# A fused sigmoid-attention and SwiGLU kernel: first unit in two parts, a refitted scheduler model, four units loaded ahead of the weights

## The chip, the cores and the metric

The kernel runs on one core of a Trainium2 chip. The metric is the device time of one execution in microseconds (us); lower is better. A comparison takes the executions of the same rounds on the same chip. The kernel before took 443.03 us (median of 3, 442.38 to 443.8).

## The reference, cut to what matters

```python
# q, k, v: (8, 12, 448, 64) float32
scores = q @ k.T / sqrt(64) - log(448)
attn   = 1 / (1 + exp(-scores))            # a sigmoid, no softmax
x      = (attn @ v) as (3584, 768)         # heads side by side
g, val = x @ w_gate, x @ w_val             # (768, 1536) each
out    = (g * sigmoid(g) * val) @ w_out    # (1536, 768)
```

The work falls into 24 **units** of four heads; three units make one batch's input of the feed-forward part.

## The kernel before: the parts that matter

A unit is loaded in three transfers (q, k, v; a transfer is a DMA) and cast to 16 bits. q and k of the first six units are transposed on TensorE (PE) and copied from PSUM, the buffers that hold TensorE's results here; those of the later units go through a DMA transpose. In the profiles PEld is TensorE's loading of weights, DVE is VectorE, POOL is GpSimd and SP issues most of the transfers. Then come seven score groups of four 64 x 64 matmuls, each with its sigmoid on ScalarE (ACT), and 28 small matmuls with v (P·V), evicted as the tiles `xT`. Feed-forward group `f` of a batch takes six gate and six value matmuls of 128 x 128 weights.

```python
slots = {"A": 2, "TO": 2, "G": 2, "st": 11, "src": 2, "v16": 3, "qkT": 3, ...}   # buffers of each kind
# A: scores.  TO: transposes, P.V and outputs share these two.  G: gate and value.  st: staging of loads.

ORDER = "q1 q2 w0 q3 w1 q4 w2 q5 w3 q6".split()     # q3: unit 3's loads; w0: a quarter of gate and value weights

loads(0)
cast_qk(0, "q", None, [("DVE", 0, 4), ("ACT", 4, NS)])
tr_pe(0, 0)
cast_qk(0, "k", None, [("DVE", 0, 4), ("ACT", 4, NS)])
tr_pe(0, 1)
```

Every operation is an object with an engine, a modelled duration, what it depends on and which buffers it takes and gives. A list scheduler in the program plays these through on a model of the core and fixes the order in which each engine's instructions are issued. So a constant of the model is no time: it can only change an order.

```python
LAT = {"PE": 0.2, "ACT": 0.1, "DVE": 0.08, "POOL": 0.25, "SP": 2.2}
...
for o in list_schedule(ops, slots, window):   # sorted by modelled start
    o.fn()
```

## Time and profile before

| | before |
|---|---|
| time, median of 3 | 443.03 us |
| span of the profiled execution | 441.6 us |
| TensorE busy / idle in it | 424.7 / 16.9 us |
| first sigmoid | 8.20 us |
| third unit's last sigmoid ends, fourth unit's first starts | 30.75, 34.13 us |
| first whole feed-forward group starts | 34.45 us |

The prediction below shows the views that carry this. Beside them stand three rows of the timeline of the kernel before (start, length, engine, line, operation; in brackets the idle time just before and what ended it). They are the place where the fourth unit comes late:

```profile
31.84 0.94 PE L282 MATMUL ps_tr<-idn,src 128*128 128x128 bf16 x14 [0.66 <-ACT xT L195]
...
34.13 1.90 ACT L329 ACTIVATE pt<-ps_sc,sbiast 128x896 f16<-128x896 f32 x2 [0.40 <-PE ps_sc L315]
34.45 1.29 PE L381 MATMUL ps_g<-xT,wg 128*128 128x448 f16 x6 [0.24 <-DVE t L391]
```

The fourth unit's 14 transposes wait for the third unit's eviction on ACT, since both need the two shared PSUM buffers. ACT therefore has no scores for over 3 us, and TensorE itself pauses twice.

### The profile page before, as it was taken

To read this page: it belongs to the slowest core of one execution; us is meant where nothing else is said; L and a number is where in the kernel's file an instruction comes from. 1 tells how busy PE (TensorE), PEld (TensorE's weight loads), DVE (VectorE), ACT (ScalarE), POOL (GpSimd) and SP (SyncE) were. 2 spreads that over 40 slices of the span, in tenths; PEclk is the share of its full clock that TensorE was granted. 3 is DMA by queue.
4 is the path that set the end of the run, shared out by engine and by line. 5 is a ranking of instruction groups with operands and counts; after the bars stand their busy time and mean duration, and the time that the engine had idled before them with its cause. 6 is when DMAs were issued, how large, how long until landed. Compare 5 with 4: busy or idle time off the path is not lost.

```text
span 441.6 us, 7888 instructions
## 1 busy us (share of the span) xinstructions
PE 424.7 (96%) x3252; PEld 211.4 (48%) x3252; DVE 168.5 (38%) x278; ACT 224.9 (51%) x305; POOL 127.8 (29%) x193
## 2 busy tenths in 40 slices
PE   3879999999999999999999999999999999999995
PEld 1444444444555545444455444544444545554563
DVE  2425543454343333434343423434333433344210
ACT  4787778756464464546545465365654452111111
POOL 2688746643230431304322403404100000000000
PEclk9999999999999999999999999999999999999999
DMA  8999989998077275265666644535410111120144
GB/s 280 378 377 376 323 251 309 309 307 255 1 203 167 72 203 127 78 133 121 154 141 115 186 106 120 181 49 165 68 37 11 27 37 37 36 71 1 43 101 108
DMA packets 64196, 66.97 MB, mean 152 GB/s; under 512 B 35488, under 2 KB 60320, under 8 KB 64160
## 3 DMA queue, kind: packets, MB, share of 16 engines
q1 hardware_dynamic: 62432, 59.39, 47.5%
q0 software_dynamic: 1728, 7.08, 7.1%
q8 instruction: 25, 0.41, 0.4%
q14 instruction: 11, 0.09, 0.1%
HBM read 47.19 MB, written 11.01 MB: 132 GB/s over the span
## 4 chain that ended last, share of the span: by engine, by line
PE 92%; ACT 3%; DMA 2%; DVE 1%; issue 1%; SPq 0%; ACTq 0%
PE ps_g L381 25%; PE ps_v L381 25%; PE ps_o L439 19%; PE ps_sc L315 9%; PE ps_pv L347 7%; PE ps_ol L439 5%; ACT pt L329 2%; DMA st_q<-in_q_dram 2%; PE ps_tr L282 1%; DVE t L391 1%; ACT s L387 1%; SPq L211 0%; DVE src L197 0%; ACT xT L195 0%; DVE osb L452 0%
## 5 line engine op out<-in xcount | busy, mean ns | idle before, releaser
L329 ACT ACTIVATE pt<-ps_sc,sbiast 128x896 f16<-128x896 f32 x168 | 159.3, 1005 | 26.1 <-PE ps_sc L315 26.0
L381 PE MATMUL ps_g<-xT,wg 128*128 128x448 f16 x576 | 125.0, 353 | 1.1 <-DVE t L391 1.0
L381 PE MATMUL ps_v<-xT,wv 128*128 128x448 f16 x576 | 125.5, 354 | 0.0
L387 ACT ACTIVATE s<-ps_g 128x448 f16<-128x448 f32 x96 | 52.2, 543 | 120.7 <-PE ps_g L381 120.7
L391 DVE TENSOR_TENSOR t<-ps_g,s 128x448 f16<-128x448 f32 x96 | 59.9, 624 | 125.5 <-ACT s L387 125.5
L439 PE MATMUL ps_o<-wo,hT 128*128 128x384 f16 x528 | 92.5, 326 | 0.0
L439 PEld LDWEIGHTS <-hT 128*128 128x128 f16 x672 | 65.7, 98 | 45.8
L397 DVE SCALAR_TENSOR_TENSOR hT<-ps_v,t 128x448 f16<-128x448 f32 x96 | 59.9, 624 | 60.2 <-PE ps_v L381 58.5
L381 PEld LDWEIGHTS <-wg 128*128 128x128 f16 x576 | 54.7, 98 | 56.7 <-issue 9.6
L381 PEld LDWEIGHTS <-wv 128*128 128x128 f16 x576 | 51.0, 98 | 61.7 <-issue 22.2
L460 POOL DMA_DIRECT2D out_dram<-osb x36 | 18.7, 525 | 134.6 <-issue 112.4
L315 PE MATMUL ps_sc<-qkT 64*64 64x448 bf16 x672 | 51.9, 374 | 4.0 <-ACT pt L329 3.2
L199 POOL CAST v<-st_v 64x448 f16<-64x448 f32 (+1 forms) x72 | 41.0, 569 | 32.6 <-PE ps_pv L347 17.6
L347 PE MATMUL ps_pv<-pt,v 64*64 64x448 f16 x672 | 38.4, 360 | 0.6 <-ACT pt L329 0.5
L199 POOL CAST src<-st_q 128x896 bf16<-128x896 f32 x21 | 19.6, 931 | 59.9 <-DMA st_q<-in_q_dram 38.2
L197 DVE CAST xT<-ps_pv 128x448 f16<-128x448 f32 x40 | 23.4, 619 | 22.9 <-PE ps_pv L347 22.9
L315 PEld LDWEIGHTS <-qkT 64*64 64x64 bf16 x672 | 14.2, 107 | 36.0 <-issue 33.4
L450 ACT ACTIVATE osb<-ps_o 128x384 f32<-128x384 f32 x22 | 10.8, 490 | 39.8 <-PE ps_o L439 39.8
L347 PEld LDWEIGHTS <-v 64*64 64x64 f16 x672 | 19.9, 109 | 15.7 <-issue 5.2
L439 PE MATMUL ps_ol<-wo,hT 128*128 128x384 f16 x144 | 24.7, 326 | 0.0
L452 DVE TENSOR_SCALAR osb<-ps_o 128x384 f32<-128x384 f32 x22 | 12.3, 557 | 31.8 <-PE ps_o L439 31.8
L199 POOL CAST src<-st_k 128x896 bf16<-128x896 f32 x21 | 19.6, 932 | 5.0 <-DMA st_k<-in_k_dram 4.3
(22 smaller groups left out, 68.7 us busy)
## 6 DMA issues: line engine op xcount, KB each, us to landing
st_q<-in_q_dram SPq DMA_DIRECT2D x24, 448.0 KB, 5.0
st_k<-in_k_dram SPq DMA_DIRECT2D x24, 448.0 KB, 5.2
st_v<-in_v_dram SPq DMA_DIRECT2D x24, 448.0 KB, 5.9
out_dram<-osb POOLq DMA_DIRECT2D x36, 192.0 KB, 3.1
st_wg<-in_moe_w_gate_dram SPq DMA_DIRECT2D x12, 384.0 KB, 8.8
st_wv<-in_moe_w_val_dram SPq DMA_DIRECT2D x12, 384.0 KB, 8.8
st_wo<-in_moe_w_out_dram SPq DMA_DIRECT2D x12, 384.0 KB, 6.8
out_dram<-osb SPq DMA_DIRECT2D x18, 192.0 KB, 2.7
```

The lines of the kernel that those rows point to most:

```text
L197: nc.vector.tensor_copy(out=o, in_=i)
L199: nc.gpsimd.tensor_copy(out=o, in_=i)
L315: nc.tensor.matmul(out=sc[64 * (g ^ a):64 * (g ^ a) + 64, a, 0:S].rearrange("k (s p) -> k s p", s=NS), lhsT=kT[r, s, 64 * g:64 * g + 64], ...
L329: nc.scalar.activation(out=pt, in_=T[("sc",) + key][:, :, 0:S], func=SIGM, bias=sb_t, scale=qkscale)
L347: nc.tensor.matmul(out=T["pv", i, a][64 * g:64 * g + 64, :], lhsT=T["v16", i][r, a, s, :], rhs=T["pt", i, s][r, a, :], start=(s == 0), sto ...
L381: nc.tensor.matmul(out=T[nm, b, f], lhsT=w[c][:, j, ff * 128:(ff + 1) * 128], rhs=T["xT", b, j], start=(j == 0), stop=(j == KC - 1))
L387: nc.scalar.activation(out=t, in_=T["g", b, f], func=SIGM)
L391: nc.vector.tensor_tensor(out=t, in0=T["g", b, f], in1=T["s16", b, f], op=MULT)
L397: nc.vector.scalar_tensor_tensor(out=T["hT", m, f][:, o * S:(o + 1) * S], in0=T["v", b, f], scalar=HSC, in1=T["t1", b, f], op0=MULT, op1=MULT)
L439: nc.tensor.matmul(out=o, lhsT=T["hT", m, f][:, t * 128:(t + 1) * 128], rhs=wo16[f][:, cs], start=(f == 0), stop=(f == NF - 1))
L452: nc.vector.tensor_scalar_mul(T["osb", m, t][:, c], o, HREC)
L460: dma.dma_start(out=out[rows, c].rearrange("(p s) d -> s p d", s=NS)[s], in_=T["osb", m, t][64 * n:64 * n + 64, c])
```

## The change

Its intent is to start earlier and to have attention work at hand while the first weights are still on their way. It has four parts.

**Split.** The first unit's k is loaded in two parts, its second half is cast on POOL, and transposes and copies go by parts, so that the first scores need only three sevenths of k.

```diff
-            load(i, nm, src)
+            load(i, nm, src, [0, 3, NS] if i == 0 and nm == "k" else None)
...
-    cast_qk(0, "q", None, [("DVE", 0, 4), ("ACT", 4, NS)])
-    tr_pe(0, 0)
-    cast_qk(0, "k", None, [("DVE", 0, 4), ("ACT", 4, NS)])
-    tr_pe(0, 1)
+    cast_qk(0, "q", None, [("DVE", 0, 4, 0), ("ACT", 4, NS, 0)])
+    tr_pe(0, 0, [("DVE", 0, 4), ("ACT", 4, NS)])
+    cast_qk(0, "k", None, [("DVE", 0, 3, 0), ("POOL", 3, NS, 1)])
+    tr_pe(0, 1, [("DVE", 0, 3), ("DVE", 3, NS)])
```

**Model.** Latencies, durations and the cost of a transfer are refitted (about a dozen more like these).

```diff
-LAT = {"PE": 0.2, "ACT": 0.1, "DVE": 0.08, "POOL": 0.25, "SP": 2.2}
-SWITCH = 0.1
+LAT = {"PE": 0.2, "ACT": 0.15, "DVE": 0.13, "POOL": 0.25, "SP": 2.2}
+SWITCH = 0.094
...
+    R["st_v", 0][0].dma += 1.5
```

**Loading order** and **issue order.** Four units stand ahead of the first weights; P·V of the first units is issued a slot later, and the fourth unit's transposes between the third's scores, no longer after its P·V.

```diff
-ORDER = "q1 q2 w0 q3 w1 q4 w2 q5 w3 q6".split()
+ORDER = "q1 q2 q3 w0 q4 w1 w2 q5 w3 q6".split()
...
-            if sl == 3 and i < QB:
+            if sl == 0 and 0 < i < QB:
+                pv(i - 1)
+            if sl == 3 and i == QB - 1:
                 pv(i)
-            if att and i + 1 < NPE:
-                if i == QB - 1:
-                    if sl == 3:
-                        tr_pe(i + 1, 0)
-                        tr_pe(i + 1, 1)
-                elif sl in (1, 2):
-                    tr_pe(i + 1, sl - 1)
+            if att and i + 1 < NPE and sl in (1, 2):
+                tr_pe(i + 1, sl - 1)
```

More of the change, by code (lines that the diff above doesn't have):

```diff
@@ L36, in __init__ @@
         self.hold = n == 1792
-        self.dma = 2.0 if n == 1792 else n / 16 * max(0.042, 0.0105 + size / 27200)
+        self.dma = 2.0 if n == 1792 else n / 16 * max(0.042, 0.0093 + size / 28700)
     def got(self, tag):
         return [s for s in self.take if s.tag == tag]
-LAT = {"PE": 0.2, "ACT": 0.1, "DVE": 0.08, "POOL": 0.25, "SP": 2.2}
-SWITCH = 0.1
+LAT = {"PE": 0.2, "ACT": 0.15, "DVE": 0.13, "POOL": 0.25, "SP": 2.2}
+SWITCH = 0.094
 START = {"SP": 0.75, "POOL": 1.4, "DVE": 3.4, "ACT": 0.75}
-ORDER = "q1 q2 w0 q3 w1 q4 w2 q5 w3 q6".split()
+ORDER = "q1 q2 q3 w0 q4 w1 w2 q5 w3 q6".split()
 AHEAD = 7
@@ L203, with load, part, fn @@
     R = {}
-    def load(i, nm, src):
+    def load(i, nm, src, cuts=None):
         b, r = divmod(i, QB)
-        def fn():
-            T["st_" + nm, i] = stg.tile([128, 2, NS, D], FP32, tag="st", bufs=slots["st"], name=f"st_{nm}{i}")
-            nc.sync.dma_start(
-                out=T["st_" + nm, i].rearrange("q a s d -> q a (s d)"),
-                in_=src[b][4 * r:4 * r + 4].rearrange("(a g) (p s) d -> (g p) a (s d)", a=2, s=NS))
-        R["st_" + nm, i] = [op("SP", 0.5, fn, take=["st"], desc=(256, NS * D * 4))]
+        def part(s0, s1):
+            def fn():
+                if s0 == 0:
+                    T["st_" + nm, i] = stg.tile([128, 2, NS, D], FP32, tag="st", bufs=slots["st"],
+                                                name=f"st_{nm}{i}")
+                nc.sync.dma_start(
+                    out=T["st_" + nm, i][:, :, s0:s1].rearrange("q a s d -> q a (s d)"),
+                    in_=src[b][4 * r:4 * r + 4].rearrange("(a g) (p s) d -> (g p) a (s d)", a=2, s=NS)
+                    [:, :, s0 * D:s1 * D])
+            return op("SP", 0.5, fn, take=["st"] if s0 == 0 else [], desc=(256, (s1 - s0) * D * 4))
+        cuts = cuts or [0, NS]
+        R["st_" + nm, i] = [part(*c) for c in zip(cuts, cuts[1:])]
     def cast_qk(i, nm, eng, parts=None):
         n = "qk".index(nm)
-        parts = parts or [(eng, 0, NS)]
+        parts = parts or [(eng, 0, NS, -1)]
         def fn(e, s0, s1):
@@ L223, in fn @@
                               T["st_" + nm, i][:, :, s0:s1])
+        one = {"DVE": 0.65, "ACT": 0.95, "POOL": 0.95}
         R["c" + nm, i] = [
-            op(e, (1.05 if e == "DVE" else 0.98) * (s1 - s0) / NS, fn(e, s0, s1), deps=R["st_" + nm, i],
+            op(e, 0.07 + one[e] * (s1 - s0) / NS, fn(e, s0, s1), deps=[R["st_" + nm, i][ld]],
                take=["src"] if nm == "q" and s0 == 0 else [],
                give=R["st_" + nm, i][0].take if s1 == NS else [])
-            for e, s0, s1 in parts]
+            for e, s0, s1, ld in parts]
     def cast_v(i, eng):
@@ L236, in fn @@
                 cp(eng, t[64 - 64 * g:128 - 64 * g, 1], T["st_v", i][64 * g:64 * g + 64, 1])
-        R["v16", i] = op(eng, 1.75, fn, deps=R["st_v", i], take=["v16"], give=R["st_v", i][0].take)
+        R["v16", i] = op(eng, 1.9, fn, deps=R["st_v", i], take=["v16"], give=R["st_v", i][0].take)
     def load_w(w, dst, c, j2, nm):
@@ L275, in qkT_tile, with tr_pe, fpe, fn @@
         T["qkT", i] = sb.tile([128, 2, NS, 128], BF16, tag="qkT", bufs=slots["qkT"], name=f"qkT_{i}")
-    def tr_pe(i, n):
-        def fpe():
-            ps = T["tr", i, n] = psum.tile([128, NS, 128], BF16, tag="TO", bufs=2, name="ps_tr")
-            for s in range(NS):
-                nc.tensor.transpose(out=ps[:, s, :],
-                                    in_=src16[i % NSRC][:, n, s].rearrange("p a d -> p (a d)"), identity=idn)
-        def fm():
-            if n == 0:
-                qkT_tile(i)
-            nc.vector.tensor_copy(out=T["qkT", i][:, n], in_=T["tr", i, n])
-        a = op("PE", 0.4, fpe, deps=R[("cq", "ck")[n], i], take=["TO"],
-               give=R["cq", i][0].take if n else [])
-        m = op("DVE", 0.62, fm, deps=[a], take=["qkT"] if n == 0 else [], give=a.take)
-        R.setdefault(("qkT", i), []).append(m)
+    def tr_pe(i, n, parts=None):
+        ins = R[("cq", "ck")[n], i]
+        parts = parts or [("DVE", 0, NS)]
+        def fpe(s0, s1):
+            def fn():
+                if s0 == 0:
+                    T["tr", i, n] = psum.tile([128, NS, 128], BF16, tag="TO", bufs=2, name="ps_tr")
+                for s in range(s0, s1):
+                    nc.tensor.transpose(out=T["tr", i, n][:, s, :],
+                                        in_=src16[i % NSRC][:, n, s].rearrange("p a d -> p (a d)"),
+                                        identity=idn)
+            return fn
+        def fm(eng, s0, s1):
+            def fn():
+                if n == 0 and s0 == 0:
+                    qkT_tile(i)
+                cp(eng, T["qkT", i][:, n, s0:s1], T["tr", i, n][:, s0:s1])
+            return fn
+        for k, (eng, s0, s1) in enumerate(parts):
+            a = op("PE", 0.06 * (s1 - s0), fpe(s0, s1), deps=[ins[min(k, len(ins) - 1)]],
+                   take=["TO"] if s0 == 0 else [], give=R["cq", i][0].take if n and s1 == NS else [])
+            if s0 == 0:
+                bank = a.take
+            m = op(eng, 0.1 + (0.53 if eng == "DVE" else 0.8) * (s1 - s0) / NS, fm(eng, s0, s1), deps=[a],
+                   take=["qkT"] if n == 0 and s0 == 0 else [], give=bank if s1 == NS else [])
+            R.setdefault(("qkT", i), []).append(m)
+            R["qkT", i, n, s0] = m
     def tr_dma(i):
@@ L320, in burst @@
         give = [x for i, s in ds if s == NS - 1 for x in R["qkT", i][0].got("qkT")]
-        a = op("PE", 0.19 * len(ds), fpe, deps=[x for i in {i for i, _ in ds} for x in R["qkT", i]],
+        deps = [x for i in {i for i, _ in ds} for x in R["qkT", i]]
+        if ds[0][0] == 0:
+            deps = [x for k, x in R.items() if k[:2] == ("qkT", 0) and len(k) > 2 and (k[2] == 0 or k[3] <= ds[0][1])]
+        a = op("PE", 0.03 + 0.19 * len(ds), fpe, deps=deps,
                mode=("Q", "Q"), take=["A"] * len(ds), give=give)
@@ L331, in fn @@
             T[("pt",) + key] = pt
-        R[("pt",) + key] = op("ACT", 0.95, fn, deps=[a], take=["pt"], give=[slot])
+        R[("pt",) + key] = op("ACT", 0.89, fn, deps=[a], take=["pt"], give=[slot])
     def pv(i):
@@ L369, in pv @@
         for g in range(2):
-            R["xT", b, 2 * r + g] = op(eng[g], 0.62, fx(g), deps=[a], take=["xT"], give=[banks[g]])
+            R["xT", b, 2 * r + g] = op(eng[g], 0.54, fx(g), deps=[a], take=["xT"], give=[banks[g]])
     def f1(b, f):
@@ L410, in f1 @@
         g, bank = product(wg16, "g", [])
-        s = op("ACT", 0.5, fs, deps=[g])
-        t = op("DVE", 0.6, ft, deps=[s], give=bank)
+        s = op("ACT", 0.45, fs, deps=[g])
+        t = op("DVE", 0.54, ft, deps=[s], give=bank)
         def val():
@@ L419, in val @@
             old = [R["f2", m - 2]] if m >= 2 and b % 2 == 0 else []
-            R["hT", b, f] = op("DVE", 0.62, fh, deps=[vv, t] + old, give=bank)
+            R["hT", b, f] = op("DVE", 0.54, fh, deps=[vv, t] + old, give=bank)
         return val
```

## The prediction

The landing of k's first part at "about 4.8" is 4.09 + 0.57 = 4.66 and an allowance of 0.1 us. The 0.15 us for a change between 64-row and full matmuls is my estimate from the round at 40.98.

"Half clock", or "cold clock", is told by durations here: in the kernel before, seven transposes took 0.93 us at 4.58 and 0.56 us at 20.27, while the granted-clock column read 1.00 for both.

> **What bounds the kernel now.** I read the page first: busy shares, then the forty slices.
>
> ```profile
> PE 424.7 (96%) x3252; PEld 211.4 (48%) x3252; DVE 168.5 (38%) x278; ACT 224.9 (51%) x305; POOL 127.8 (29%) x193
> ...
> PE   3879999999999999999999999999999999999995
> ...
> DMA  8999989998077275265666644535410111120144
> ```
>
> TensorE is busy 424.7 of 441.6 us, so it waits 16.9 us in all. The row of slices (11 us each) shows where: the first three and the last. Nothing that leaves the matmuls alone can save more than those gaps and some cold clock. Next I cut the span at the events that matter (columns: stretch, length, then busy time of PE, PEld, DVE, ACT, POOL, granted clock, DMA share, GB/s):
>
> ```profile
> 4.58:8.20 3.62, 2.49 (x22) 1.68 (x23) 1.58 (x3) 0.54 (x3) 0.00 (x0) 1.00 0.96 311
> 8.20:14.60 6.40, 4.10 (x34) 1.99 (x30) 3.04 (x5) 4.83 (x6) 4.00 (x6) 1.00 1.05 383
> 14.60:20.00 5.40, 5.37 (x55) 3.08 (x54) 1.78 (x3) 4.15 (x5) 3.86 (x7) 1.00 1.07 373
> 20.00:26.30 6.30, 4.49 (x68) 2.28 (x67) 2.40 (x4) 6.30 (x8) 4.91 (x7) 1.00 1.06 377
> 26.30:33.60 7.30, 6.07 (x70) 3.07 (x66) 1.78 (x3) 5.21 (x7) 6.24 (x10) 1.00 1.06 377
> 33.60:60.00 26.40, 26.09 (x243) 12.52 (x244) 14.48 (x24) 18.99 (x25) 20.23 (x27) 1.00 0.92 305
> ```
>
> Length less PE busy gives idle: 1.13, 2.30, 0.03, 1.81, 1.23 and 0.31 us, together 6.8. To these come 4.58 us before the first transpose and 5.1 us of the last 32.6, where only the last evictions and writes remain. From 33.6 us on TensorE practically never waits. The waits say for whom, and the timeline where (start, length, engine, line; in brackets the idle time before and its releaser):
>
> ```profile
> PE ps_tr L282 <- DVE src L197: 5.8, 3, 4.6
> PE ps_sc L315 <- ACT pt L329: 3.2, 6, 0.7
> ...
> 8.20 2.80 ACT L329 ACTIVATE pt<-ps_sc,sbiast 128x896 f16<-128x896 f32 x3 [2.26 <-PE ps_sc L315]
> 8.87 2.19 POOL L199 CAST v<-st_v 128x448 f16<-128x448 f32 x3 [7.53 <-DMA st_v<-in_v_dram]
> ...
> 10.02 0.63 DVE L197 CAST src<-st_q 128x896 bf16<-128x896 f32 x1 [2.52 <-DMA st_q<-in_q_dram]
> ...
> 17.51 11.17 ACT L329 ACTIVATE pt<-ps_sc,sbiast 128x896 f16<-128x896 f32 x12 [1.13 <-PE ps_sc L315]
> ...
> 19.09 0.67 PEld L282 LDWEIGHTS <-src 128*128 128x128 bf16 x7 [0.38 <-DVE xT L197]
> ...
> 20.27 0.56 PE L282 MATMUL ps_tr<-idn,src 128*128 128x128 bf16 x7
> ```
>
> So the head is a chain: load, cast, transpose, copy, scores, sigmoid; then one sigmoid per 0.93 us (11.17 over 12), 6.5 us per unit of seven, beside DMA at full rate. The first feed-forward matmul stands at 26.31. The first unit's sigmoids start at 8.20, the second's only at 17.51, and the third's end at 30.75. Then ACT starts no sigmoid until 34.13, because the fourth unit is transposed at 31.84, after the third unit's output is evicted.
>
> [...]the granted-clock column reads 1.00: seven transposes took 0.93 us at 4.58 and at 19.09, 0.56 us at 20.27. TensorE was first busy without a gap from 14.63. [...]here a cast of 896 elements took 0.93 us on POOL and 0.63 on DVE.
>
> **The change part by part.** The order of instructions in the built program shows TensorE's count unchanged; SP, POOL and DVE get one instruction more each. Tensor work is only moved.
>
> *First unit in parts.* The whole k landed at 5.43, 1.34 us after q at 4.09. The first 3/7 of it should land 0.57 us after q[...], about 4.8. DVE's cast of 384 elements, interpolated from 0.43 us for 512 and 0.63 for 896, is 0.36 us: done at 5.2. TensorE finishes q's transposes at 5.51 as before (0.93 us from 4.58), then takes three of k, 0.4 us at that clock: 5.9. Add 0.26 us, the distance from 5.51 to the copy at 5.77, and some 0.35 us for half a copy: 6.5. Scores start at about 6.6 in place of 7.56, the first sigmoid at about 7.2 in place of 8.20. Gain **1.0 us** at that point. q's copy, shared by DVE and ACT, ends near 6.25 and doesn't bind. POOL's cast of the rest of k, 4/7 of 0.93, costs nothing: POOL was idle to 8.87.
>
> *What is left of it at the second unit.* Its q still lands at about 10.0 and its k at 11.2, since as many bytes lie ahead of them. Before, the second unit's first scores stood behind five steps of the first unit's P·V (14.96 to 17.1); now two score groups stand ahead of it. Transposes of k at 12.6 to 13.5, copy to 14.3, scores to 14.9: first sigmoid near 15.0, 2.5 us earlier. But P·V then starts at 15.3, still at half clock (20 matmuls 2.1 us), and with two score tiles in PSUM the third sigmoid waits until about 18.0: the lead is two sigmoids (1.9 us) less 0.5. The two banks shared by P·V, transposes and outputs bring small waits again before the fourth and fifth. By the end of the second unit I have 23.7 where the kernel before had 24.0. So most of the first lead is spent: TensorE at half clock, not the load, limits 14 to 20 us. I keep **0.3 us**, with up to 1.5 if the bank waits are milder.
>
> *Four units ahead of the weights.* q3 moves ahead of the first weight chunk. By landings of 1.2 us per unit tensor (10.02, 11.22, 12.54) and 1.0 per weight tile, the fourth unit lands from 17.4 to 19.8, not 23.6 to 26.05, and the chunk from 20.8 to 25.9, not up to 22.35. Casting its last piece ends near 26.7. The value product wants it after that and moves behind the third unit's P·V in the order; the gate product needs its half by 28, cast by 24.1. In return the fourth unit is transposed between the third's scores, in gaps where TensorE waited for ACT (1.81 us of 6.30), and its first two score groups run as soon as the third unit's sigmoids end. So the 3.4 us without sigmoids shrink to under 1. Work that stood on the saturated path after 31.84 disappears from it: the fourth unit's 14 transposes (0.94 us) and eight score matmuls (0.57 us). Against that, four value matmuls (0.93 us) move from a gap to the busy stretch. Adding a wait of 0.24 us at 34.45 that goes: 0.94 + 0.57 - 0.93 + 0.24, about 0.8, and up to 1.6 if the value matmuls too fall beside the evictions: I take **1.5 us**.
>
> *The refitted model.* It reorders everything, but from 33.6 to 409 us there are 1.1 us of idle, 1.0 of them before gate products late in the kernel, and that part of the order is unchanged (the last 100 groups of matmuls, of 367, are the same). Changes between 64-row and full matmuls on TensorE are 182, not 180; four more lie in the head, so two fewer later. One round of scores, gate and value takes 2.97 us at 40.98; 12 matmuls of 0.19 and the 0.38 of two groups' streams would be 2.7, so a change costs about 0.15 us. Two fewer: **0.3 us**.
>
> Sum: 0.3 + 1.5 + 0.3 = 2.1; half of the milder case, another 0.4, makes 2.5 us.
>
> **Rivals.** (1) *The whole head moves.* If TensorE reaches full clock[...] earlier, the second unit keeps its 2.5 us, and with the fourth unit's 1.5 the gain is 4 to 5: about 438.5. For it: all idle stretches named sum to 6.8 us. [...](2) *The wait moves.* Landings lose 2.2 us between k at 5.43 and v at 8.87 (3.44 us for one tensor, where 1.2 is usual). If that stall catches the second half of k, its four transposes, which stand before the second score group, block TensorE to about 9 and the second sigmoid by 1.7 us. With the weights also 3.5 us later, the gain is eaten: 442.5 to 443.5.[...] (3) *POOL becomes the bound.* For a unit it takes 0.93 + 0.93 + 1.78 = 3.64 us, as DMA does. It is late by some 1.8 us with v3, and may hold the first weight cast; a late value product would cost 1 us. The later chunks have slack: the second was cast by 33.1, its first gate product at 40.98.
>
> **Range and chances.** Before is 443.03, so I predict 440.5 us. Rival 1 with some luck gives 437.8; rival 2 and the spread of before (442.38 to 443.8) give 443.2. Faster by 2% would take 8.9 us, more than the 6.8 us of idle that can be touched: 0.02. Slower by 2% would need a new wait inside the saturated 350 us; nothing points to one: 0.01. Within 2%: 0.97.
>
> **What would show it right or wrong.** Right: first sigmoid near 7.2; second unit's first near 15, its third near 18; sigmoids almost without a gap from the third unit to the fourth; idle of TensorE over the span near 14.5 us. Wrong: a first sigmoid after 7.8, or a gap after it, would say the halves of k landed late. Transposes at 0.56 us per seven before 18 us would mean the clock rose early (rival 1). TensorE waiting for POOL or a weight load at the first value product is rival 3. Idle between 34 and 400 us above 2 us would say that the refit misplaced the order.

## The result and the profile after

The changed kernel took 440.89 us (median of 6, 440.62 to 440.97), the kernel before 442.29 us (median of 6, the three more runs included). A ratio in this text is the mean time of one kernel's executions over that of the other's in the same rounds, so it is not quite the ratio of the medians. Here it is 0.9963, with a 95% interval of 0.9947 to 0.9978: 1.6 us of 442. A second measurement on another occasion (e9 below) gave 440.42 us and 0.9947 (0.9931 to 0.9963), or 2.3 us.

The busy shares on the page of the changed kernel:

```profile
PE 424.7 (97%) x3252; PEld 211.1 (48%) x3252; DVE 168.5 (38%) x279; ACT 225.1 (51%) x305; POOL 128.1 (29%) x194
```

In this execution TensorE is busy exactly as long as before (in e9 below, the same program, it is not: 422.6 us). The span of this execution is 439.1 us, so all of the 2.5 us between the two profiled executions is idle time: 14.4 in place of 16.9 us. The same stretches as in the prediction (length, busy time of PE, PEld, DVE, ACT, POOL, granted clock, DMA share, GB/s):

```profile
4.58:8.20 3.62, 2.87 (x26) 1.73 (x27) 1.47 (x4) 1.53 (x3) 1.20 (x3) 1.00 1.01 350
8.20:14.60 6.40, 4.89 (x42) 2.33 (x45) 3.08 (x6) 5.57 (x6) 3.17 (x5) 1.00 1.05 386
14.60:20.00 5.40, 5.05 (x55) 2.35 (x48) 1.96 (x4) 3.92 (x4) 4.88 (x8) 1.00 1.07 378
20.00:26.30 6.30, 5.22 (x81) 3.10 (x78) 3.09 (x6) 6.11 (x7) 5.22 (x7) 1.00 1.05 375
26.30:33.60 7.30, 6.57 (x80) 3.46 (x80) 2.30 (x5) 6.43 (x9) 6.38 (x9) 1.00 1.07 373
33.60:60.00 26.40, 26.30 (x231) 12.26 (x230) 13.54 (x23) 19.20 (x26) 18.72 (x25) 1.00 0.97 315
```

Idle by stretch is now 0.75, 1.51, 0.35, 1.08, 0.73 and 0.10 us, 4.5 in place of 6.8. The timeline of the head:

```profile
7.09 4.77 ACT L353 ACTIVATE pt<-ps_sc,sbiast 128x896 f16<-128x896 f32 x5 [0.68 <-PE ps_sc L336]
...
14.72 1.91 ACT L353 ACTIVATE pt<-ps_sc,sbiast 128x896 f16<-128x896 f32 x2 [0.68 <-PE ps_sc L336]
14.82 2.08 PE L371 MATMUL ps_pv<-pt,v 64*64 64x448 f16 x20
...
17.33 1.01 ACT L353 ACTIVATE pt<-ps_sc,sbiast 128x896 f16<-128x896 f32 x1 [0.71 <-PE ps_sc L336]
...
20.19 9.13 ACT L353 ACTIVATE pt<-ps_sc,sbiast 128x896 f16<-128x896 f32 x10 [0.67 <-PE ps_sc L336]
...
30.25 1.91 ACT L353 ACTIVATE pt<-ps_sc,sbiast 128x896 f16<-128x896 f32 x2
```

The first unit's sigmoids start at 7.09. The second unit's start at 14.72, but P·V then takes TensorE for 2.08 us, 0.10 us per small matmul, so the third of them waits until 17.33. From 20.19 ten run without a gap, and the third unit's last ends at 29.32 (30.75 before). The fourth unit's first starts at 30.25, 0.9 us later and not 3.4. The first whole feed-forward group starts at 33.38, where it was 34.45, and by then TensorE has done the fourth unit's second score pair and the fifth's transposes as well, which stood after it before.

### The profile page after: what moved, and what is told of

It is laid out like the page before. It is cut to its first block, busy times and chain, and to the rows that moved or that the text cites. A ratio compares the mean times of both kernels' runs of the same rounds, so it can differ in the third digit from the quotient of the medians.

```text
span 439.1 us, 7892 instructions
## 1 busy us (share of the span) xinstructions
PE 424.7 (97%) x3252; PEld 211.1 (48%) x3252; DVE 168.5 (38%) x279; ACT 225.1 (51%) x305; POOL 128.1 (29%) x194
## 4 chain that ended last, share of the span: by engine, by line
PE 93%; ACT 3%; DVE 2%; DMA 1%; issue 1%; ACTq 0%
PE ps_g L405 25%; PE ps_v L405 25%; PE ps_o L463 20%; PE ps_sc L336 9%; PE ps_pv L371 8%; PE ps_ol L463 5%; ACT pt L353 2%; PE ps_tr L294 1%; DVE t L415 1%; DMA st_q<-in_q_dram 1%; ACT s L411 1%; DVE qkT L197 0%; DVE xT L197 0%; ACT qkT L195 0%; DVE src L197 0%
## 5 line engine op out<-in xcount | busy, mean ns | idle before, releaser
L199 POOL CAST src<-st_k 128x896 bf16<-128x896 f32 (+1 forms) x22 | 20.2, 918 | 8.6 <-DMA st_k<-in_k_dram 8.4
```

The lines of the kernel that those rows point to most:

```text
L199: nc.gpsimd.tensor_copy(out=o, in_=i)
```

## The experiments

Twelve kernels were run, in three sets (e1 to e4, e5 to e8, e9 to e12) with five timed rounds each, every set on a chip of its own. All gave correct results. All ratios are to the kernel before, in the rounds of the set; kernels of different sets are compared by these ratios. "First" and "second" measurement of the changed kernel mean 0.9963 and 0.9947.

### e1: the first unit whole again

```diff
-            load(i, nm, src, [0, 3, NS] if i == 0 and nm == "k" else None)
+            load(i, nm, src)
...
-    tr_pe(0, 0, [("DVE", 0, 4), ("ACT", 4, NS)])
+    tr_pe(0, 0)
-    cast_qk(0, "k", None, [("DVE", 0, 3, 0), ("POOL", 3, NS, 1)])
-    tr_pe(0, 1, [("DVE", 0, 3), ("DVE", 3, NS)])
+    cast_qk(0, "k", None, [("DVE", 0, 4, 0), ("ACT", 4, NS, 0)])
+    tr_pe(0, 1)
```

> The changed kernel with the first unit loaded, cast, transposed and copied whole again; loading order, issue order and refitted model kept. My theory (the lead of the early start is mostly spent at half clock between 14 and 20 us): first sigmoid back to 8.0 to 8.2 us from 7.09, but only 0.3 to 0.6 us slower in all than the changed kernel, about 441.3. Rival (each microsecond of the head reaches the end): 1.0 us slower or more, 441.9. A third possibility, that the split does nothing for the end: 440.9.

Measured: 440.26 us, ratio 0.9942 (0.9929 to 0.9956). The first sigmoid came at 8.13, and yet the kernel is not seen to be slower than with the split: of my three cases, the third is the nearest. A loss of 0.3 us (0.0007) is less than these intervals resolve. The timeline of e1 shows a second difference:

```profile
13.49 14.81 ACT L353 ACTIVATE pt<-ps_sc,sbiast 128x896 f16<-128x896 f32 x16 [0.37 <-PE ps_sc L336]
...
13.60 1.66 PE L371 MATMUL ps_pv<-pt,v 64*64 64x448 f16 x20
```

The same 20 matmuls take 1.66 us here and 1.14 at full clock (as in e1 itself at 20.34), 2.08 in the first profile of the changed kernel. So by these durations the clock rose while they ran, near 14.7 us (an estimate), some 5 us earlier than in that profile, and 16 sigmoids ran without a gap; the third unit's last ended at 28.30. In e1 TensorE's work ran on without a pause from 10.61 us, as nothing waited between the second unit's transposes and the P·V; in the first profile it paused for 0.72 us before its scores at 14.08. That the pause delayed the clock is not shown by this pair: e9 below has the same pause of 0.72 us and an early clock. So the profiles of e1 and of the first measurement differ in the clock as well as in the split; e9 is the fairer partner for e1.

### e2: the old model

```diff
-LAT = {"PE": 0.2, "ACT": 0.15, "DVE": 0.13, "POOL": 0.25, "SP": 2.2}
-SWITCH = 0.094
+LAT = {"PE": 0.2, "ACT": 0.1, "DVE": 0.08, "POOL": 0.25, "SP": 2.2}
+SWITCH = 0.1
...
-        R[("pt",) + key] = op("ACT", 0.89, fn, deps=[a], take=["pt"], give=[slot])
+        R[("pt",) + key] = op("ACT", 0.95, fn, deps=[a], take=["pt"], give=[slot])
```

(and the other durations likewise)

> The changed kernel with the scheduler's old latencies and durations (only the cast durations stay, without which the split can't be ordered). 316 of 6507 TensorE rows move. My theory: the refit is worth 0.3 us through two fewer mode changes, so 441.2. Rival: the refit places nothing that matters, 440.9 within 0.2; second rival: it is the larger part of the gain, 442 or more, and the profile shows new idle time of TensorE between 34 and 400 us.

Measured: 440.98 us, 0.9955 (0.9939 to 0.9971), between the two measurements of the changed kernel. No part of the gain can be seen to come from the refit.

### e3 and e8: the old orders

e3 undoes the loading order and the issue order, e8 the issue order alone. The edits are the last diff of the change, backwards.

> The changed kernel with the old loading order (three units, then the first weights) and the old issue order of P.V and of the fourth unit's transposes. My theory: the fourth unit's sigmoids start 1 us or more after the third's end, and 1.0 to 1.5 us are lost, 442.0 to 442.4. Rival (the whole lead comes from the early start and landings): under 0.4 us lost, 441.2.

> The changed kernel with the old issue order of P.V and of the fourth unit's transposes, but the new loading order: tells which half of e3's 1.5 us it is. Theory: the new loading order alone gives nothing, since the fourth unit is then transposed only after the third's P.V: 442.0 to 442.5. Rival: the loading order alone is enough, 440.9 to 441.2.

Measured: e3 442.43 us, 0.9987 (0.9972 to 1.0001); e8 442.03 us, 0.9978 (0.9960 to 0.9996). Without the two orders most of the gain is gone: 0.0024 of 442 us, or 1.1 us, against the first measurement of the changed kernel, 0.0040 or 1.8 us against the second. In the mean the new loading order without the issue order brings little; the difference of e8 to e3 lies within the intervals. The timeline of e3:

```profile
17.25 12.78 ACT L353 ACTIVATE pt<-ps_sc,sbiast 128x896 f16<-128x896 f32 x14 [2.24 <-PE ps_sc L336]
...
31.12 0.94 PE L294 MATMUL ps_tr<-idn,src 128*128 128x128 bf16 x14 [0.66 <-ACT xT L195]
```

This profile of e3 is of its slowest execution (442.90 us). It is the picture of the kernel before: sigmoids without a gap to 30.03, then the fourth unit's transposes wait for the third's eviction, and ACT gets its next scores at 33.48. The split was in, and the first sigmoid came at 7.31; by the end of the third unit its lead over the kernel before was 0.7 us. In e8 the fourth unit's loads are early, and it comes late all the same:

```profile
31.82 0.94 PE L294 MATMUL ps_tr<-idn,src 128*128 128x128 bf16 x14 [0.66 <-ACT xT L195]
...
34.34 1.90 ACT L353 ACTIVATE pt<-ps_sc,sbiast 128x896 f16<-128x896 f32 x2 [0.61 <-PE ps_sc L336]
```

The third unit's last sigmoid ended at 30.25, 4.1 us before. This too is the slowest of the kernel's executions (442.86 us); two of its six, at 440.78 and 440.86, are as fast as the changed kernel, so how much e8 loses is not settled. The reverse, the new issue order with the old loading order, was not run: whether the issue order alone would do stays open.

### e4: TensorE kept busy before the first data

```diff
     loads(0)
+    warm_pe(27)      # 27 matmuls of the identity on itself, into a PSUM buffer not needed before 26 us
```

> The changed kernel with 27 matmuls of the identity on itself on TensorE ahead of the first transposes (from about 1.4 to 4.3 us, where it is idle), into a PSUM buffer not needed before 26 us; the order of all other instructions is the same. My theory (TensorE at half clock limits the stretch to 20 us): seven transposes take 0.56 us from about 8 us on or earlier, the third sigmoid of the second unit comes at about 16.6 in place of 17.33, the gaps of ACT before 20 us close, and the end comes 1 to 2 us earlier, 439 to 440. Rival (landings and ACT set that stretch): the clock rises early, but the end stays within 0.4 us of 440.9.

Measured: 441.13 us, 0.9959 (0.9941 to 0.9976). In the profiled execution the clock did not rise early: seven transposes still took 0.93 us at 11.80 and 13.59, 0.56 us only at 20.83. Its mean granted clock is 1.000, but that of the other five executions is 0.984 to 0.992, while no execution of a kernel without filler is under 0.997. In e6 below this column reads 1.00 while ten transposes take 1.27 us at 4.57, and 0.50 only after the clock has risen and fallen (seven in 0.93 us at 10.36). If it reads so here too, the clock had risen and fallen again in those five. So e4 tests nothing about what an early clock is worth. It shows something else: POOL's cast of the second half of k, which waits for that load, started at 7.48 us and not at 5.95, and the second sigmoid waited 1.16 us. That is rival 2 of the prediction. The cast started at 6.74 in e2, 7.29 in e3 and 7.20 in e8, and at 5.95 and 6.10 in the two profiles of the changed kernel. Why this load lands so unevenly stays open.

### e5, e6, e7: busy through the first transposes

The same kind of filler in three kernels: e5 is e1 with it, e6 the changed kernel, e7 the kernel before (e5 and e7 have two more matmuls between the two groups of transposes). The scheduler gives it no time, and all other instructions keep their order (compared instruction by instruction). That the clock would be up by about 8 us with it, as the expectations here and in e4 have it, was my assumption; no run before had shown it.

```diff
     loads(0)
+    warm_pe(30)
...
+    warm_pe(6, R["qkT", 0][2].deps[0], True)    # e6: six more after the last of the first ten transposes
```

> The kernel of e1 (first unit whole) with TensorE kept busy by 30, 2 and 6 matmuls of the identity before, between and after the first unit's two groups of transposes, from 1.4 to about 7.4 us; the order of all else is that of e1. In e4 27 such matmuls did not raise the clock (seven transposes still 0.93 us at 11.80)[...]. Theory[...]: by 8.3 us the clock is up, seven transposes at 10.6 take 0.56 us, P.V of the first unit 1.1 us for 20, sigmoids run without a gap of over 0.3 us from the second unit on, and the time is 438.8 to 439.8. Rival (landings set that stretch): the clock is up early but the time stays at 440.3 within 0.3.

> The changed kernel with 30 such matmuls before its first transposes and 6 after them, order of all else kept. Theory: the clock is up by about 8 us if the second half of k lands before 7 us, and the time is 439.0 to 440.0, 1 us or more under 440.9; where that half lands late, the second sigmoid waits as in e4 and part of it is lost. Rival: no change, 440.9.

> The kernel before with the matmuls of e5. Theory: half clock costs it less, since its sigmoids already run without a gap from 17.51 us and its fourth unit comes late whatever the clock; 0.5 to 1 us faster than before, ratio 0.998 to 0.999. Rival (the clock alone is worth as much as the change): 1.5 us or more, ratio 0.9965 or less.

Measured: e5 440.89 us, 0.9953 (0.9936 to 0.9970); e6 440.09 us, 0.9940 (0.9925 to 0.9954); e7 443.65 us, 1.0015 (0.9998 to 1.0032). All three missed what I expected, e6 only just. The clock did rise by 7.5 us in all three: four transposes at 7.09 took 0.40 us in e6, 0.61 us in the changed kernel; eight score matmuls took 0.57 us at 7.69 in e5 and at 7.51 in e7, 0.96 us at 7.56 in the kernel before. But it fell again. Three windows of e6 (columns as above; the third from the end is the granted clock):

```profile
8.00:9.00 1.00, 0.45 (x8) 0.17 (x8) 0.00 (x0) 1.00 (x2) 0.56 (x2) 1.00 1.05 384
9.00:10.00 1.00, 0.49 (x8) 0.18 (x7) 0.46 (x1) 1.00 (x2) 0.94 (x2) 0.77 1.02 382
10.00:11.00 1.00, 1.00 (x11) 0.65 (x7) 0.41 (x2) 1.00 (x2) 0.59 (x1) 0.50 1.05 394
```

TensorE was busy for about half of 8 to 10 us, and the granted clock went to 0.50 within this time, at about 9.5 us; it was back at about 12.9 us (0.53 from 12 to 13, then 1.00). Seven transposes at 10.36 took 0.93 us, so this is the same half clock as in the head of the other kernels. In e5 it was back only at about 16 us (0.50 up to 16, 0.94 from 16 to 17), in e7 at about 20 (0.50 from 19 to 20, 0.85 from 20 to 21), as late as in the kernel before. e5 and e7 are therefore inconclusive about what an early clock is worth. In e6 the second and third units' 14 sigmoids ran without a gap from 14.23, and the first whole feed-forward group started at 31.02, 2.4 us before the first profile of the changed kernel; but the span fell by only 1.2 us, to 437.9. Between 33.6 and 60 us TensorE idled 1.26 us in place of 0.10: at 44.09 it waited for POOL's cast of the sixth unit, whose load had only just landed.

### e9 to e12: the sixth unit's load

e9 is the changed kernel again. e10 moves the sixth unit's loads ahead of the third weight chunk; TensorE's order stays the same. e11 is e10 with the filler of e6. e12 adds three groups of four filler matmuls in the gaps from 8 to 10.4 us. (By the windows above the clock of e6 fell at about 9.5, not at 9.8 as the expectation of e12 has it.)

```diff
-ORDER = "q1 q2 q3 w0 q4 w1 w2 q5 w3 q6".split()
+ORDER = "q1 q2 q3 w0 q4 w1 q5 w2 w3 q6".split()
...
             for ds in bursts(i, sl):
                 burst(ds)
+                if ds[0] in ((0, 2), (0, 3), (0, 4)):     # e12 only
+                    warm_pe(4, R["pt", 0, ds[0][1]].deps[0], ds[0][1] == 4)
```

> The changed kernel itself, for comparison in the same rounds as e10 to e12: ratio to before 0.995 to 0.997, as in the first measurement (0.9963).

> The changed kernel with the sixth unit's three loads ahead of the third weight chunk; TensorE's order is the same, ten rows of POOL and nine of SP change places. In e6 TensorE reached the sixth unit's transposes early and waited 1.16 us at 44.09 for POOL's cast of it, which waited for the load. In the changed kernel it gets there later and has 0.1 us of idle time between 33.6 and 60 us. Theory (this wait exists only for a kernel that is ahead): no change, within 0.3 us of e9. Rival (the load order costs something already): 0.5 us faster or more.

> e6 (the changed kernel with TensorE kept busy through the first transposes) and e10 together. Theory: the clock gives 2.4 us in the head, of which e6 gave back 1.2 at the sixth unit; without that wait it is 2 us faster than e9, about 438.9, ratio 0.991 to 0.992, with under 0.4 us of idle between 33.6 and 60 us. Rival (the wait only moves to the third weight chunk): within 0.3 us of e6's ratio of 0.994.

> e11 with three groups of four more such matmuls after the third, fourth and fifth score groups, in the gaps from 8 to 10.4 us after which the clock fell again at about 9.8 us in e6. Theory: the clock stays up, seven transposes at 10.4 take 0.56 us, and the second unit's first sigmoid comes 0.3 to 0.5 us earlier: 0 to 0.5 us faster than e11, since ACT is then the limit. Rival: the extra matmuls delay score groups and cost 0.2 to 0.4 us.

Measured in the same rounds: e9 440.42 us, 0.9947 (0.9931 to 0.9963), just under what I expected; e10 440.75 us, 0.9944 (0.9925 to 0.9963); e11 439.85 us, 0.9932 (0.9917 to 0.9947); e12 439.33 us, 0.9916 (0.9900 to 0.9931). The means of e9 and e10 are both 440.5; e12's is 439.25, 1.2 us less than the changed kernel.

e9 is the most telling of all, since its program is that of the changed kernel. Its timeline:

```profile
13.94 0.57 PE L336 MATMUL ps_sc<-qkT 64*64 64x448 bf16 x8 [0.72 <-ACT pt L353]
14.37 12.71 ACT L353 ACTIVATE pt<-ps_sc,sbiast 128x896 f16<-128x896 f32 x14 [0.48 <-PE ps_sc L336]
```

Its waits from 33.6 to 60 us (who waits, for what, total us, count, longest):

```profile
PE ps_tr L294 <- POOL src L199: 1.1, 1, 1.1
```

And the same stretch as a window:

```profile
33.60:60.00 26.40, 25.19 (x224) 11.70 (x224) 12.95 (x22) 18.27 (x23) 19.20 (x26) 1.00 0.95 311
```

In this execution the clock had risen by 13.94: eight score matmuls took 0.57 us, where they took 0.96 at 14.08 in the first profile. With that, the gaps of the second unit are gone, and the first whole feed-forward group starts at 31.16, 2.2 us earlier than in the first profile of the same program. The span is 438.1 and not 439.1 us: 1.0 of the 2.2 us is kept, and 1.1 comes back as a wait for the sixth unit at 44.17. TensorE's idle time from 33.6 to 60 us is 1.21 us in place of 0.10. Its busy time in the whole span is 422.6 us, not 424.7, which fits the shorter matmuls of the second unit (20 of P·V took 1.11 us at 14.34, 2.08 at 14.82 in the first profile), and its idle time is 15.5 us.

Beside e1, whose profile had an early clock too, e9 does show the lead of the split: the third unit's sigmoids end at 27.08, where e1 has 28.30, and the first whole group starts at 31.16, where e1 has 32.74. But e1 does not wait between 33.6 and 60 us, and the spans are 438.1 and 438.4 us. That would be the 0.3 us that the prediction kept. It is one profile of each, on two chips, so it is a hint and not shown.

With the sixth unit early and the clock up from 4.4 us (e12: seven transposes in 0.55 us at 4.44), the wait moves once more. The timeline of e12, and one line of its waits after it:

```profile
6.56 6.48 ACT L353 ACTIVATE pt<-ps_sc,sbiast 128x896 f16<-128x896 f32 x7 [0.48 <-PE ps_sc L336]
...
13.33 12.72 ACT L353 ACTIVATE pt<-ps_sc,sbiast 128x896 f16<-128x896 f32 x14 [0.29 <-PE ps_sc L336]
```

```profile
PE ps_sc L336 <- DMA qkT<-src: 1.4, 1, 1.4
```

ACT runs almost without a gap from 6.56 to 26, and the first whole group starts at 30.24. But at 59.87 TensorE waits 1.4 us for the seventh unit, whose q lands at 53.6 and which goes through a DMA transpose. e11's profile had such a wait of 0.9 us at 59.98. So e11 fell short of the 438.9 us I had expected, in part by something like my own rival: the wait moved, though to the seventh unit and not to the third weight chunk. The other part is the clock. In e11's profile, its fastest execution (439.43 us), the clock stayed up: seven transposes at 10.55 took 0.56 us, although TensorE was busy for only 38% of each microsecond from 8 to 10, less than in e6 (45 and 49%), where it fell: the busy share of these two microseconds alone does not tell the two apart. In its other five executions the mean granted clock is 0.988 to 0.995, so there it probably fell, as in all five of e6 (0.992 to 0.994). In e12 it is 0.997 or more in all five: the filler in the gaps may have held it up. And e10 alone changes nothing, as expected. e12 is the fastest kernel here; it beats the changed kernel of the same rounds by 0.3%, and the kernel before by 0.8%.

## Why the prediction was right, and where not

It said 440.5 us; 440.89 and 440.42 were measured, inside 437.8 to 443.2. "Within 2%" held, and the reason given was the right one: only idle time in the head, and some matmuls at half clock (seven transposes in 0.93 us in place of 0.56), could be had. Idle over the span was to be near 14.5 us and was 14.4 with TensorE's work at 424.7 us; in e9 it was 15.5 us with 422.6 us of work. That the number itself came so near is partly luck. The base moved: with three more runs the kernel before went from 443.03 to 442.29, and against that 1.6 us were gained at first, 2.3 us in the second measurement, not 2.5. And the sum is softer than it looks: the term for the four units is worked out as "about 0.8, and up to 1.6" and then taken as 1.5, and the last 0.4 us belong to no term of their own. With 0.8 and without the 0.4 the same terms give 1.4 us. The terms fared differently.

- **First sigmoid near 7.2 us:** 7.09 and 6.96. Second unit's first near 15: 14.72.
- **The split, 0.3 us, up to 1.5 (the cause failed, the size is open).** The step "TensorE at half clock, not the load, limits 14 to 20 us" was right for the first profile: the third sigmoid waited to 17.33, I had said 18.0. But I took the clock's rise near 20 us for a property of the program. It is not: the same program had its full clock at 13.94 in e9. Nor was 14.63 the start of the first busy stretch without a gap in the kernel before: its own timeline has one from 10.70 to 13.90. The timed rounds show no gain from the split, since the ratio without it (e1) is 0.9942; as much as 1.5 us (0.0034) is hard to fit with that, but 0.3 us (0.0007) is not resolved. The profiles of e9 and e1, both with an early clock, differ by 0.3 us in the span; there 1.1 us of the lead of 1.6 us at the first whole group went into the wait for the sixth unit, and in e9 nothing was lost at half clock between 14 and 20 us (20 of P·V in 1.11 us at 14.34).
- **Four units ahead, 1.5 us:** right in mechanism and size. Undoing both orders (e3) costs 1.1 to 1.8 us; the pause of the sigmoids went from 3.4 to 0.9 us, as said. That the size came out is in part the choice of 1.5 from "0.8 to 1.6". I had not told the two orders apart; e8's timeline shows the fourth unit late in spite of early loads, so the loading order alone does not remove the pause. Its time is too scattered to say more, and the issue order alone was not tried.
- **The refit, 0.3 us:** not seen (e2). Two mode changes fewer, 0.15 us each by my estimate, are below what five rounds resolve.
- **Rival 1, full clock earlier, 438.5:** its premise came true in e9 (full clock by 13.94, near 20 us in the first profile), its number didn't. The step that failed is the sum: a lead in the head (2.5 us in the prediction, 2.2 in e9) was simply added to the end. What the prediction overlooked is that loads set the pace behind the head, with DMA at a share of 0.97 from 33.6 to 60 us. In e9 TensorE waited 1.1 us for the sixth unit at 44 us, in e11 and e12 0.9 and 1.4 us for the seventh at 60.
- **Rival 2, the second half of k late:** it happens (e3, e4, e8) and cost a sigmoid 0.8, 1.2 and 1.0 us, but not in the two profiles of the changed kernel.
- **Rival 3, POOL as the bound of the first value product:** not seen. Its last weight piece was cast by 26.1, the product started at 30.06 without waiting for it.

What stays open: when exactly the clock rises in an execution of a given program, and with it why the kernel before scatters over 2.3 us (441.74 to 444.07 in all sets) and the changed one over 1.2 us. With the same 30 filler matmuls in front from 1.40 us on, seven transposes took 0.55 us at 4.44 in e12, ten took 1.27 us at 4.57 in e6, and seven 0.93 us at 4.66 in e11, where three took 0.40 us at 5.91. e12, whose clock is up from 4.4 us in the profile, scatters over 0.5 us (five executions); that fits, but one profile per kernel does not prove it. Open too is how often the changed kernel has the early clock of e9's profile: that execution (439.82 us) was the fastest of its six, and the one profiled in the first measurement (440.92 us) was like the other five.

## What to carry to other kernels

Before a gain in the head of a kernel is added to the end, follow the next thing that arrives at a fixed time: here 2.2 us won in the head (e9) met the sixth unit's load (the cast of its q started at 42.82 in the first profile, at 43.18 in e9), and half of it came back as a wait 13 us later; in e12 a wait came 30 us later. Reordering so that independent work stands at hand where an engine waits was worth 1.1 to 1.8 us, where no gain from the earlier start was resolved. And two profiles of one program can differ in the head by the moment at which TensorE's clock rises (by 13.94 us in e9, near 20 us in the first profile of the same program). So judge a change there by timed rounds, or try filler work in both, and look at the granted clock of every execution: with e12's filler its mean was 0.997 or more in all five, with e6's 0.992 to 0.994.
